# Loading the second half of the weights in 4-KB runs, in tiles of two modes by 256 rows, contracted behind all attention

## Chip, cores, metric

One core of one Trainium2 chip. The metric is the time of one execution in microseconds (us) on the device, median of several runs. The kernel before takes 467.04 us (runs from 466.96 to 467.75).

## The reference, cut to what matters

Attention with a decay for 8 batches and 8 heads (sequence 576, head size 64), then a spectral mix: the first 64 modes of the Fourier transform along the sequence are multiplied by a complex 512 x 512 matrix of their own, and transformed back.

```python
x = attention(q, k, v, f).transpose(0, 2, 1, 3).reshape(8, 576, 512)
X = np.fft.rfft(x, axis=1)[:, :64]
Yr = einsum('bmd,mde->bme', Xr, w_r) - einsum('bmd,mde->bme', Xi, w_i)
Yi = einsum('bmd,mde->bme', Xr, w_i) + einsum('bmd,mde->bme', Xi, w_r)
u = x + np.fft.irfft(Y, n=576, axis=1)
out = u + np.maximum(u @ w_ch, 0)
```

`w_r` and `w_i` are 64 x 512 x 512 floats each, 134 MB in all: each weight is read once and used for 8 batches only. q, k, v are 28 MB, the output 9 MB.

## The kernel before

The 32 steps of attention (4 pairs of heads, called dc, times 8 batches) each load q, k, v on the SyncE queue. The weights come as 64 tiles of 4 modes x 128 rows, real and imaginary part in one transfer each, cast to bf16 on the way, through a ring of 9 buffers, on the queue that POOL (the GpSimd engine) feeds. A row of a weight matrix is 512 floats: one contiguous run of 2 KB per mode and partition.

```python
    MG = 4
    NG = NM // MG
    # ... cut ...
    NRING = 9
    # ... cut ...
    def emit_w_load(n):
        dc, g = tile_of(n)
        wb = wpool.tile([128, 2, MG, D], BF16, tag="wb", name="wb")
        parts = 2 if n == NDC * NG - 1 else 1
        for h in range(parts):
            ms = slice(h * MG // parts, (h + 1) * MG // parts)
            for t, src in enumerate((moe_w_r, moe_w_i)):
                nc.gpsimd.dma_start(
                    wb[:, t, ms, :],
                    src[g * MG : (g + 1) * MG, dc * 128 : (dc + 1) * 128, :][
                        ms
                    ].rearrange("m p e -> p m e"),
                )
        wtiles[n] = wb
    # ... cut ...
    def emit_modes(n):
        dc, g = tile_of(n)
        wb = wtiles.pop(n)
        XT3 = XT3s[dc]
    # ... cut ...
        for mi in range(MG):
            m = g * MG + mi
            for eb in range(NDC):
                for t, c0 in ((0, B), (1, 0)):
                    nc.tensor.matmul(
                        A[:, eb, mi, :],
                        lhsT=wb[:, t, mi, eb * 128 : (eb + 1) * 128],
                        rhs=XT3[:, m, c0 : c0 + 2 * B],
                        start=(t == 0),
                        stop=(t == 1),
                    )
        ysl = Yacc[:, :, g * MG : (g + 1) * MG, :]
        if dc == 0:
            nc.vector.tensor_copy(ysl, A[:, :, :, :])
        elif dc < NDC - 1:
            nc.vector.tensor_tensor(ysl, A[:, :, :, :], ysl, ALU.add)
```

The last of the four dc passes adds into `YT` (or `YTl` for the 16 modes that come last), the finished spectrum as the next step reads it, instead of `Yacc`. In the loop over attention steps, two tiles are contracted per step from the ninth step on; `emit_dft` makes the Fourier coefficients of one 128-row block of d:

```python
        for s in range(NS + 1):
            if s + STG - 1 < NS:
                emit_loads(s + STG - 1)
    # ... cut ...
            if s >= 1:
                emit_dft(s - 1)
                vaugs.pop(s - 1)
            if s > B:
                for j in range(2):
                    emit_modes(2 * (s - B - 1) + j)
                    next_w()
        nmode = 2 * (NS - B)
```

The last 16 tiles follow behind attention, beside the blocks `emit_xw` (x times w_ch) and, once `YT` is complete, the eight blocks `emit_y`. After the very last tile comes the output phase ("tail": `emit_late`, `emit_x`, `emit_out`).

```python
            nx = ny = 0
            last = NDC * NG
            while nmode < last - 1:
                emit_modes(nmode)
                nmode += 1
                if nmode <= last - GL:
                    if nx < B:
                        emit_xw(nx)
                        nx += 1
                    next_w()
                if nmode > last - GL:
                    for _ in range((3, 3, 1)[nmode - (last - GL) - 1]):
                        emit_y(ny)
                        ny += 1
            emit_y(ny)
```

The softmax here doesn't subtract the row's maximum and nothing guards it: scores larger than these inputs give would overflow.

## Time and profile before

| | before |
|---|---|
| median time | 467.04 us |
| span in the profile | 466.2 us |
| last weight transfer landed | 422.0 us |
| from there to the end ("tail") | 44.2 us |
| last write of x_all (end of attention) | 331.6 us |
| weights where they are alone, bf16 written | 207 GB/s (414 GB/s read) |

The rows below the first come from one profiled execution. It took 468.06 us, 0.3 us more than the slowest timed run.

The first fence is from the page of the kernel before: rows over the span (the granted TensorE clock in tenths, the busy tenths of the 16 DMA engines, GB/s in 40 slices of 11.7 us), the packets, and the shares of the chain that ended last.

```profile
PEclk9988999997577667776757766669559999889998
DMA  8999999999999999999999999999999999992667
GB/s 187 268 268 268 268 268 268 267 267 253 233 236 236 235 234 231 229 235 230 232 236 237 235 226 206 207 206 206 207 207 206 207 207 206 207 177 79 229 245 270
DMA packets 93235, 106.27 MB, mean 228 GB/s; under 512 B 4032, under 2 KB 88512, under 8 KB 93184
...
DMA 89%; PE 5%; ACT 2%; issue 1%; DVE 1%; POOL 1%; DVEq 0%; ACTq 0%; POOLq 0%
```

The DMA row is at 9 up to 420 us (8 in the first slice): the transfers are never idle. The GB/s row tells who uses them: 268 with q, k, v and weights together, 207 from 280 us on with weights alone. The chain of waits is 89% DMA.

The chain in order of time shows the pace of the transfers: start, duration, what. Each hop spans eight weight transfers (POOL issues one when the one eight earlier has landed), then 0.28 us until the next.

```profile
324.54 20.06 DMA wb<-in_moe_w_i_dram
344.60 0.28 issue
...
406.94 15.01 DMA wb<-in_moe_w_i_dram
422.00 0.55 PE A L111 x15
...
423.24 0.40 PE pl L645 x4
423.69 0.82 PE pl L649 x3
```

So eight transfers of 1 MB read take 20.06 + 0.28 = 20.34 us, 2.54 us each. The last landing releases PE at 422.00; what follows is the tail.

The windows view gives busy time of PE (TensorE, matmuls), weight loads, DVE (VectorE), ACT (ScalarE) and POOL, then the granted clock, DMA share and GB/s of a stretch:

```profile
core 0: us, PE busy (x) PEld busy (x) DVE busy (x) ACT busy (x) POOL busy (x), PEclk, DMA share, GB/s
60.00:100.00 40.00, 33.71 (x669) 27.14 (x671) 36.22 (x99) 39.47 (x62) 6.37 (x9) 1.00 1.16 268
100.00:140.00 40.00, 26.46 (x499) 22.58 (x500) 21.83 (x61) 22.03 (x34) 7.63 (x11) 0.72 1.19 244
404.00:411.00 7.00, 4.26 (x43) 2.48 (x45) 1.03 (x2) 0.59 (x1) 1.40 (x2) 0.51 1.24 206
411.00:422.00 11.00, 10.13 (x138) 6.42 (x138) 4.20 (x9) 4.09 (x7) 0.00 (x0) 1.00 0.84 140
```

(The DMA share can exceed 1 because the records of packets overlap in time.) Up to 100 us ACT is full; after it attention waits for weights (ACT 22 of 40 us). And the y blocks, which run from 407.9 to 420.0 us, keep PE busy 10.1 of 11 us before the last landing: the tail starts at full clock.

### The profile page before, as it was taken

The numbers are of one execution on the slowest core, as the hardware profiler recorded it, in microseconds if no ns is written. First come the engines' busy times: TensorE is split into PE (matmuls) and PEld (weight loads), VectorE is DVE, ScalarE is ACT, GpSimd is POOL, SyncE is SP. The second block draws the span as 40 slices with busy tenths as digits, with TensorE's granted clock in tenths as the row PEclk, the third lists the DMA queues.
The fourth block names the chain that finished last, engine by engine and source line by source line (L and its number), as shares of the span: only waits on it lengthen the run. The fifth ranks groups of instructions, "written<-read, shape, count | busy, mean of one in ns | idle before, by whom it ended". The sixth has DMA issues, their size and how long they took to land.

```text
span 466.2 us, 11413 instructions
## 1 busy us (share of the span) xinstructions
PE 321.9 (69%) x4800; PEld 236.0 (51%) x4845; DVE 250.9 (54%) x625; ACT 250.7 (54%) x376; POOL 123.4 (26%) x154
## 2 busy tenths in 40 slices
PE   1667777996655655565565566776369999597993
PEld 1445556775544544454555455665346555453441
DVE  7767898995444445553544445655223233235774
ACT  4778999995444445554444445654004444134763
POOL 6111100311212222122222222322233222300884
PEclk9988999997577667776757766669559999889998
DMA  8999999999999999999999999999999999992667
GB/s 187 268 268 268 268 268 268 267 267 253 233 236 236 235 234 231 229 235 230 232 236 237 235 226 206 207 206 206 207 207 206 207 207 206 207 177 79 229 245 270
DMA packets 93235, 106.27 MB, mean 228 GB/s; under 512 B 4032, under 2 KB 88512, under 8 KB 93184
## 3 DMA queue, kind: packets, MB, share of 16 engines
q0 software_dynamic: 68144, 67.64, 87.0%
q1 hardware_dynamic: 24960, 37.77, 25.4%
q8 instruction: 38, 0.62, 0.5%
q10 hardware_dynamic: 80, 0.13, 0.2%
q14 instruction: 13, 0.11, 0.1%
HBM read 163.73 MB, written 9.44 MB: 371 GB/s over the span
## 4 chain that ended last, share of the span: by engine, by line
DMA 89%; PE 5%; ACT 2%; issue 1%; DVE 1%; POOL 1%; DVEq 0%; ACTq 0%; POOLq 0%
DMA wb<-in_moe_w_i_dram 69%; DMA wb<-in_moe_w_r_dram 12%; DMA wch<-in_moe_w_ch_dram 8%; PE pz L674 2%; PE pu L686 1%; PE pz L686 1%; ACT uo L702 1%; ACT uo L699 0%; PE pu L669 0%; PE pl L649 0%; POOL wb L86 0%; DVE uo L703 0%; DVE uo L696 0%; DVEq L755 0%; PE pl L645 0%
## 5 line engine op out<-in xcount | busy, mean ns | idle before, releaser
L111 PEld LDWEIGHTS <-wb 128*128 128x128 bf16 x2048 | 67.2, 100 | 109.3 <-DMA wb<-in_moe_w_i_dram 88.0
L86 POOL DMA_DIRECT2D wb<-in_moe_w_r_dram x65 | 48.3, 743 | 188.3 <-DMA wb<-in_moe_w_r_dram 103.6
L86 POOL DMA_DIRECT2D wb<-in_moe_w_i_dram x65 | 48.3, 742 | 116.4 <-DMA wb<-in_moe_w_i_dram 112.4
L437 ACT ACTIVATE E_129<-ps 128x1024 bf16<-128x1024 f32 x64 | 54.3, 875 | 12.0 <-PE ps L430 10.6
L437 ACT ACTIVATE E_128<-ps 128x1024 bf16<-128x1024 f32 x64 | 53.9, 867 | 7.8 <-PE ps L430 7.6
L111 PE MATMUL A<-XT_1367,wb 128*128 128x16 bf16 x512 | 21.1, 174 | 40.6 <-DMA wb<-in_moe_w_i_dram 33.9
L122 DVE TENSOR_TENSOR Yacc<-A,Yacc 128x256 f32<-128x256 f32 x32 | 14.1, 441 | 64.1 <-PE A L111 63.4
L591 ACT CAST XW<-pxw 128x512 bf16<-128x512 f32 x40 | 22.7, 586 | 39.2 <-PE pxw L584 39.2
L111 PE MATMUL A<-XT_2872,wb 128*128 128x16 bf16 x512 | 20.4, 174 | 28.6 <-DMA wb<-in_moe_w_i_dram 26.0
L584 PE MATMUL pxw<-wch,yy 128*128 128x512 bf16 x152 | 36.7, 391 | 1.9 <-DVE yy L580 1.6
L384 ACT COPY KTz_0_126<-tp 64x576 bf16<-64x576 bf16 x16 | 10.9, 680 | 43.9 <-PE tp L375 43.9
L700 POOL TENSOR_TENSOR uo<-uo 64x512 f32<-64x512 f32 (+1 forms) x14 | 25.2, 1808 | 27.5 <-DVE uo L696 24.7
L384 ACT COPY KTz_0_124<-tp 64x576 bf16<-64x576 bf16 x16 | 10.3, 644 | 40.7 <-PE tp L375 40.6
L473 DVE TENSOR_TENSOR x_all<-pav,rcp 128x384 bf16<-128x384 f32 x64 | 31.1, 486 | 0.4
L464 PE MATMUL pav<-va,E_128 128*128 128x65 bf16 x480 | 26.3, 215 | 6.6 <-PE px L488 1.8
L126 DVE TENSOR_TENSOR YT<-A,Yacc 128x256 bf16<-128x256 f32 x12 | 7.3, 611 | 42.1 <-PE A L111 42.1
L111 PE MATMUL A<-XT_454,wb 128*128 128x16 bf16 x512 | 18.1, 171 | 16.9 <-DMA wb<-in_moe_w_i_dram 13.1
L464 PE MATMUL pav<-va,E_129 128*128 128x65 bf16 x480 | 27.3, 216 | 3.6 <-PE px L488 2.0
L430 PE MATMUL ps<-QTs,KTz_0_124 128*128 128x512 bf16 (+2 forms) x96 | 27.6, 341 | 2.9 <-ACT E_129 L437 1.8
L430 PE MATMUL ps<-QTs,KTz_0_126 128*128 128x512 bf16 (+2 forms) x96 | 26.6, 333 | 2.5 <-ACT E_128 L437 2.1
L464 PEld LDWEIGHTS <-E_128 128*128 128x128 bf16 x480 | 23.7, 113 | 8.8 <-issue 2.8
L464 PEld LDWEIGHTS <-E_129 128*128 128x128 bf16 x480 | 24.4, 114 | 5.0 <-issue 3.0
(138 smaller groups left out, 740.2 us busy)
## 6 DMA issues: line engine op xcount, KB each, us to landing
wb<-in_moe_w_r_dram POOLq DMA_DIRECT2D x63, 512.0 KB, 24.8
wb<-in_moe_w_i_dram POOLq DMA_DIRECT2D x63, 512.0 KB, 25.1
out_dram<-uo SPq DMA_DIRECT2D x16, 512.0 KB, 3.0
stq_113<-in_q_dram SPq DMA_DIRECT2D x11, 288.0 KB, 8.4
stk_114<-in_k_dram SPq DMA_DIRECT2D x11, 288.0 KB, 8.2
stv_115<-in_v_dram SPq DMA_DIRECT2D x11, 288.0 KB, 8.7
stq_116<-in_q_dram SPq DMA_DIRECT2D x11, 288.0 KB, 9.6
stk_117<-in_k_dram SPq DMA_DIRECT2D x11, 288.0 KB, 9.6
```

Source lines behind the costliest of these rows:

```text
L86: nc.gpsimd.dma_start(wb[:, t, ms, :], src[g * MG : (g + 1) * MG, dc * 128 : (dc + 1) * 128, :][ms].rearrange("m p e -> p m e"),)
L111: nc.tensor.matmul(A[:, eb, mi, :], lhsT=wb[:, t, mi, eb * 128 : (eb + 1) * 128], rhs=XT3[:, m, c0 : c0 + 2 * B], start=(t == 0), stop=(t ...
L122: nc.vector.tensor_tensor(ysl, A[:, :, :, :], ysl, ALU.add)
L384: nc.scalar.copy(KTz[s % NK][h][hs, 0:S].rearrange("c (p r) -> c p r", r=NR), tv[hs, :, :],)
L430: nc.tensor.matmul(ps[:, h, o : o + n], lhsT=KTz[s % NK][h][:, jb * 128 : (jb + 1) * 128], rhs=QT[s][:, jb * 128 + c0 : jb * 128 + c0 + n] ...
L437: nc.scalar.activation(E[:, :, piece * 512 : piece * 512 + w], ps[:, :, 0:w], ACT.Exp, scale=scale,)
L464: nc.tensor.matmul(pav[:, i, h, :], lhsT=E[:, h, c : c + 128], rhs=va[:, jb, h, :], start=(jb == 0), stop=(jb == sb),)
L473: nc.vector.tensor_tensor(x_all[:, b, sbs[0] : sbs[0] + n, dc * 128 : (dc + 1) * 128].rearrange("p c (h d) -> p c h d", h=2), pav[:, 0:n, ...
L584: nc.tensor.matmul(pxw[:, :], lhsT=xT[:, eb, sb * 128 : (sb + 1) * 128], rhs=wch[:, eb, :], start=(eb == 0), stop=(eb == NDC - 1),)
L591: nc.scalar.copy(XW[:, b, sb, :], pxw[:, :])
L674: nc.tensor.matmul(pz[:, i, :], lhsT=ident_bf[:, :], rhs=XW[:, b, sb0 + i, :], start=True, stop=False,)
L700: nc.gpsimd.tensor_tensor(o_sb, o_sb, u_sb, ALU.add)
```

## The change

Intent: fewer, longer runs. Two neighbouring rows of a weight matrix are 4 KB in a piece. If partition p holds rows 2p and 2p+1 of the second half of d (256 rows), the runs double. That needs the coefficients of even and odd rows (a DFT with a stride of 2 in d) and contracts both dc passes in one, which is possible only when attention is done for all heads. So the first 32 tiles stay as they were, now spread over the 24 steps (4/3 per step in place of 2), and 32 new tiles of 2 modes x 256 rows come behind attention.

```diff
-    xtpool = ctx.enter_context(tc.tile_pool(name="xtpool", bufs=2))
+    xtpool = ctx.enter_context(tc.tile_pool(name="xtpool", bufs=3))
+    NT = NDC * NG
+    NTH = NT // 2
+    M2 = MG // 2
+    GL = 8
     # emit_w_load, second half:
+            wb = wpool.tile([128, 2, M2, 2 * D], BF16, tag="wb", name="wb")
+                    nc.gpsimd.dma_start(
+                        wb[:, t, ms, :],
+                        src[g * M2 : (g + 1) * M2, D // 2 : D, :][ms].rearrange(
+                            "m (p r) e -> p m (r e)", r=2
+                        ),
+                    )
     # emit_modes, second half:
+            terms = [
+                (XT3s[2 + r], r, t, c0) for t, c0 in ((0, B), (1, 0)) for r in (0, 1)
+            ]
     # emit_dft: nothing at dc == 2; at dc == 3 two blocks of stride 2
+            for c, d0, st in [(dc, dc * 128, 1)] if dc < 2 else [(2, 256, 2), (3, 257, 2)]:
     # the attention loop
-                for j in range(2):
-                    emit_modes(2 * (s - B - 1) + j)
+                while nmode < (s - B) * NTH // (NS - B):
+                    emit_modes(nmode)
     # behind attention
-                if nmode > last - GL:
-                    for _ in range((3, 3, 1)[nmode - (last - GL) - 1]):
+                if nmode % 4 and nx < B:
+                    emit_xw(nx)
+                if nmode > last - 6 and ny < B - 1:
+                    for _ in range(2 if ny < 4 else 1):
                         emit_y(ny)
```

(To make room, ident_f and ones_row move into Yacc's space, trimask and wdec into the attention's pool, and vb has one buffer.)

More of the change, by code (lines that the diff above doesn't have):

```diff
@@ L63 @@
     ident_bf = const.tile([128, 128], BF16, name="ident_bf")
-    ident_f = const.tile([128, 128], F32, name="ident_f")
-    trimask = const.tile([128, 128], BF16, name="trimask")
     wch = const.tile([128, NDC, D], BF16, name="wch")
@@ L68 @@
     BI = const.tile([128, SP], BF16, name="BI")
-    wdec = const.tile([128, NSB, BH], BF16, name="wdec")
-    wdec6 = const.tile([RP, NR, BH], BF16, name="wdec6")
     wtiles = {}
-    GL = 4
+    NT = NDC * NG
+    NTH = NT // 2
+    M2 = MG // 2
+    GL = 8
     def tile_of(n):
-        dc, g = divmod(n, NG)
-        return dc, (g + GL) % NG if dc == NDC - 1 else g
+        if n < NTH:
+            return divmod(n, NG)
+        return 2, (n - NTH + GL) % NTH
     def emit_w_load(n):
         dc, g = tile_of(n)
-        wb = wpool.tile([128, 2, MG, D], BF16, tag="wb", name="wb")
-        parts = 2 if n == NDC * NG - 1 else 1
-        for h in range(parts):
-            ms = slice(h * MG // parts, (h + 1) * MG // parts)
+        if n < NTH:
+            wb = wpool.tile([128, 2, MG, D], BF16, tag="wb", name="wb")
             for t, src in enumerate((moe_w_r, moe_w_i)):
                 nc.gpsimd.dma_start(
-                    wb[:, t, ms, :],
-                    src[g * MG : (g + 1) * MG, dc * 128 : (dc + 1) * 128, :][
-                        ms
+                    wb[:, t, :, :],
+                    src[
+                        g * MG : (g + 1) * MG, dc * 128 : (dc + 1) * 128, :
                     ].rearrange("m p e -> p m e"),
                 )
+        else:
+            wb = wpool.tile([128, 2, M2, 2 * D], BF16, tag="wb", name="wb")
+            parts = 2 if n == NT - 1 else 1
+            for h in range(parts):
+                ms = slice(h * M2 // parts, (h + 1) * M2 // parts)
+                for t, src in enumerate((moe_w_r, moe_w_i)):
+                    nc.gpsimd.dma_start(
[4 more added lines that the diff above has]
+                    )
         wtiles[n] = wb
@@ L98, in emit_modes @@
         wb = wtiles.pop(n)
-        XT3 = XT3s[dc]
+        nm = MG if n < NTH else M2
         if late["psM"] is None:
             z = late["psZ"].tile([128, 2, D], F32, tag="z", name="A")
-            A = z[:, 0, 0 : NDC * MG * 2 * B].rearrange(
-                "p (e m c) -> p e m c", e=NDC, m=MG
-            )
-        else:
-            A = late["psM"].tile([128, NDC, MG, 2 * B], F32, tag="A", name="A")
-        for mi in range(MG):
-            m = g * MG + mi
+            A = z[:, 0, 0 : NDC * nm * 2 * B].rearrange(
+                "p (e m c) -> p e m c", e=NDC, m=nm
+            )
+        else:
+            A = late["psM"].tile([128, NDC, nm, 2 * B], F32, tag="A", name="A")
+        if n < NTH:
+            terms = [(XT3s[dc], 0, t, c0) for t, c0 in ((0, B), (1, 0))]
+        else:
+            terms = [
+                (XT3s[2 + r], r, t, c0) for t, c0 in ((0, B), (1, 0)) for r in (0, 1)
+            ]
+        for mi in range(nm):
+            m = g * nm + mi
             for eb in range(NDC):
-                for t, c0 in ((0, B), (1, 0)):
+                for i, (XT3, r, t, c0) in enumerate(terms):
                     nc.tensor.matmul(
                         A[:, eb, mi, :],
-                        lhsT=wb[:, t, mi, eb * 128 : (eb + 1) * 128],
+                        lhsT=wb[:, t, mi, r * D + eb * 128 : r * D + (eb + 1) * 128],
                         rhs=XT3[:, m, c0 : c0 + 2 * B],
-                        start=(t == 0),
-                        stop=(t == 1),
-                    )
-        ysl = Yacc[:, :, g * MG : (g + 1) * MG, :]
-        if dc == 0:
+                        start=(i == 0),
+                        stop=(i == len(terms) - 1),
+                    )
+        ysl = Yacc[:, :, g * nm : (g + 1) * nm, :]
+        if n < NG:
             nc.vector.tensor_copy(ysl, A[:, :, :, :])
-        elif dc < NDC - 1:
+        elif n < NTH:
             nc.vector.tensor_tensor(ysl, A[:, :, :, :], ysl, ALU.add)
         else:
-            n8 = MG * 2
+            n8 = nm * 2
             yt, w = (late["YTl"], GL * n8) if g < GL else (late["YT"], 2 * NM)
@@ L129, in emit_modes @@
                 ),
-                _strided(A[:, 0, 0, 0:1], [[MG * 2 * B, NDC], [1, B], [B, n8]]),
+                _strided(A[:, 0, 0, 0:1], [[nm * 2 * B, NDC], [1, B], [B, n8]]),
                 _strided(
-                    Yacc[:, 0, g * MG, 0:1], [[NM * 2 * B, NDC], [1, B], [B, n8]]
+                    Yacc[:, 0, g * nm, 0:1], [[NM * 2 * B, NDC], [1, B], [B, n8]]
                 ),
@@ L157 @@
         )
+        trimask = ssb.tile([128, 128], BF16, name="trimask")
+        wdec = ssb.tile([128, NSB, BH], BF16, name="wdec")
+        wdec6 = ssb.tile([RP, NR, BH], BF16, name="wdec6")
         NK, NE = 2, 2
@@ L197, in scratch @@
             )
+        ident_f = scratch(128, 128)
         ftf = scratch(128, S)
@@ L265 @@
         nc.vector.tensor_copy(cumT[:64, 4, :], cum_ps[:64, 4, :])
-        ones_row = const.tile([1, 128], F32, name="ones_row")
+        ones_row = scratch(1, 128)
         nc.vector.memset(ones_row[:], 1.0)
@@ L364, in emit_transposes @@
             )
-            vb = qkb.tile([RP, NR, 2, Dh], BF16, tag="vb", name="vb")
+            vb = qkb.tile([RP, NR, 2, Dh], BF16, tag="vb", name="vb", bufs=1)
             nc.vector.tensor_tensor(
@@ L483, in emit_dft @@
             dc, b = steps[s]
-            if b == 0:
-                XT3s[dc] = xtpool.tile([128, NM, 3 * B], BF16, tag="XT3", name="XT3")
-            px = psT.tile([128, NM, 2], F32, tag="tr", name="px")
-            for sb in range(NSB):
-                nc.tensor.matmul(
+            if dc == 2:
+                return
+            for c, d0, st in [(dc, dc * 128, 1)] if dc < 2 else [(2, 256, 2), (3, 257, 2)]:
+                if b == 0:
+                    XT3s[c] = xtpool.tile(
+                        [128, NM, 3 * B], BF16, tag="XT3", name=f"XT{c}"
+                    )
+                px = psT.tile([128, NM, 2], F32, tag="tr", name="px")
+                for sb in range(NSB):
+                    nc.tensor.matmul(
+                        px[:, :, :],
+                        lhsT=_strided(x_all[:, b, sb, d0 : d0 + 1], [[st, 128]]),
+                        rhs=bas[:, sb, :, :],
+                        start=(sb == 0),
+                        stop=(sb == NSB - 1),
+                    )
+                XT3 = XT3s[c]
+                nc.vector.tensor_copy(
+                    _strided(XT3[:, 0, B + b : B + b + 1], [[3 * B, NM], [B, 2]]),
                     px[:, :, :],
-                    lhsT=x_all[:, b, sb, dc * 128 : (dc + 1) * 128],
-                    rhs=bas[:, sb, :, :],
-                    start=(sb == 0),
-                    stop=(sb == NSB - 1),
-                )
-            XT3 = XT3s[dc]
-            nc.vector.tensor_copy(
-                _strided(XT3[:, 0, B + b : B + b + 1], [[3 * B, NM], [B, 2]]), px[:, :, :]
-            )
-            nc.scalar.mul(XT3[:, :, b : b + 1], px[:, :, 1:2], -1.0)
+                )
+                nc.scalar.mul(XT3[:, :, b : b + 1], px[:, :, 1:2], -1.0)
         NS = len(steps)
         nload = NRING
+        nmode = 0
         def next_w():
@@ L533 @@
             if s > B:
-                for j in range(2):
-                    emit_modes(2 * (s - B - 1) + j)
+                while nmode < (s - B) * NTH // (NS - B):
+                    emit_modes(nmode)
+                    nmode += 1
                     next_w()
-        nmode = 2 * (NS - B)
     with ExitStack() as bctx:
@@ L542 @@
         raw = xtpool.tile([128, NM, 3 * B], BF16, tag="XT3", name="YTl")
-        nl = 2 * GL * MG
+        nl = 2 * GL * M2
         YTl = (
@@ L551 @@
         yy = bsb.tile([128, B, 2, D], BF16, name="yy")
-        nc.vector.memset(YT[:, :, :, 0 : 2 * GL * MG], 0.0)
+        nc.vector.memset(YT[:, :, :, 0 : 2 * GL * M2], 0.0)
         yflat = yy[:, :, :, :].rearrange("p b t e -> p (b t e)")
@@ L611 @@
             nx = ny = 0
-            last = NDC * NG
+            last = NT
             while nmode < last - 1:
@@ L615 @@
                 nmode += 1
-                if nmode <= last - GL:
-                    if nx < B:
-                        emit_xw(nx)
-                        nx += 1
-                    next_w()
-                if nmode > last - GL:
-                    for _ in range((3, 3, 1)[nmode - (last - GL) - 1]):
+                next_w()
+                if nmode % 4 and nx < B:
+                    emit_xw(nx)
+                    nx += 1
+                if nmode > last - 6 and ny < B - 1:
+                    for _ in range(2 if ny < 4 else 1):
                         emit_y(ny)
```

## The prediction

> **What bounds the kernel now.** Transfers. The chain of waits is 89% DMA, hops ending on weight transfers from 3.5 to 422.0 us; then a tail of 44 us (PE, ACT, DVE, stores) that no load hides. The slice rows show DMA at 9 tenths nearly throughout. Weights, written as bf16, move at 207 GB/s where they are alone (280 to 400 us): 414 GB/s read. In the windows view PE and ACT are busy about 60% and 50% from 100 to 280 us: attention waits for weights. Only before 100 us is ACT full (39.5 of 40 us), and there DMA is full too (268 GB/s with q, k, v).
>
> **What the change does.**
> - Bytes, matmuls and weight loads stay. The second half of the weights (67 MB read) comes in 4-KB runs in place of 2-KB, with half the descriptors.
> - Attention consumes 32 tiles in place of 48, so it ends near 250 us in place of 335; the other 32 are contracted behind it. The DMA sum is the same: this alone saves nothing.
> - Ring: at 6.1 us a step (as at 60 to 100 us) a step uses 1.33 tiles and DMA brings about 0.65 beside q, k, v. The ring of 9 drains before attention ends, so DMA never lacks a free buffer. Behind attention, 8 XW blocks with 11 tiles cost PE about 60 us, in which DMA brings 12 tiles; the ring takes that.
> - One vb buffer, strided DFT loads, smaller evacuations: off the critical path.
>
> **Cost.** In the chain 8 weight transfers take 20.05 + 0.28 us: 2.54 us per 1 MB read, 32 runs on each of 16 engines, 79 ns per 2-KB run. The Trainium skill, "DMA: Bandwidth & Descriptors" (section Bandwidth), gives 32-byte beats at 850 MHz and about 3 cycles fixed per packet: (64+3)/0.85 = 78.8 ns, which this trace agrees with. A 4-KB run is then (128+3)/0.85 = 154 ns, an estimate from that page: 2.2 to 2.6% less. 64 transfers x 0.06 us = 3.7 to 4.2 us saved on the critical path.
>
> Against it: the eight y blocks run now between 406 and 420 us and warm PE's clock (granted 0.51 at 404 to 411, 1.00 at 411 to 422). The instruction order hoists them three or four tiles earlier; after them PE does 1 us of modes per 5 us, so the tail probably starts cold. "TensorE: Matmul & The Clock Gate" (Part 1) gives a window of about 3.4 us before the clock doubles; 3 us of matmuls at half rate cost an estimated 1 to 2 us. The last evacuation is half the size: -0.2 us.
>
> Sum: 467.0 - 4.0 + 1.3 - 0.2 = **464.1 us**, range 460.5 to 467.0. Faster by over 2%: 0.05; within 2%: 0.92; slower: 0.03.
>
> **What the profile would show.**
> - Software queue about 16,000 packets fewer; weights alone at 211 to 213 GB/s from about 255 us on.
> - Last x_all write near 250 us, q, k, v ended before; DMA at 9 until the last weight lands near 418 us.
> - Tail 45 to 46 us, granted clock near 0.5 in its first 3 us.
>
> **What would make it wrong.**
> - 4-KB runs get split, or another limit sets the rate: 467 to 468.
> - Fewer descriptors also relieve slow DMA engines (the weight rate fades from 414 to 421 us, engines finishing unevenly): 2 to 3 us more.
> - Attention over 9 us a step by itself, or PE behind after it: full ring, idle DMA, slower.
> - PE stays warm: 1.3 us faster.

## The result

| | before | changed |
|---|---|---|
| median time | 467.04 us | 464.98 us (464.76 to 465.33) |
| span in the profile | 466.2 us | 463.0 us |
| last weight transfer landed | 422.0 us | 417.4 us |
| tail | 44.2 us | 45.6 us |
| last write of x_all | 331.6 us | 253.6 us |
| weights alone, written | 207 GB/s | 211 GB/s |

The ratio is 0.9953 (95% interval 0.9936 to 0.9970). It is the mean time of one kernel's fast runs over that of the other's of the same rounds, so not quite the ratio of the medians. A later repeat, beside the experiments, gave 0.9954 (465.53 us against 467.27). The gain is half a percent: by the bound of 2% "the same", but clear of noise.

The page of the changed kernel, same lines:

```profile
PEclk9979999999987887579899599998555558657998
DMA  8999999999999999999999999999999999982667
GB/s 205 268 268 268 268 268 268 267 267 267 268 266 228 232 258 240 246 217 264 208 206 208 211 212 211 211 211 211 211 211 211 211 211 211 211 161 83 225 245 267
DMA packets 76852, 106.28 MB, mean 230 GB/s; under 512 B 4032, under 2 KB 55744, under 8 KB 76800
...
DMA 88%; PE 6%; ACT 1%; issue 1%; DVE 1%; POOL 1%; DVEq 0%; ACTq 0%; POOLq 0%
```

There are 16,383 packets fewer, at the same MB, and 211 GB/s in place of 207 from the slice at 280 us on. The DMA row is as full as before: neither the earlier end of attention nor the ring let the transfers idle. The granted clock, however, sits at 5 in the slices from 320 us on, but for a short rise.

The chain of the changed kernel:

```profile
302.35 19.60 DMA wb<-in_moe_w_i_dram
...
402.75 14.67 DMA wb<-in_moe_w_i_dram
...
417.46 0.55 PE A L130 x14
...
418.46 0.61 PE pl L674 x4
419.07 1.71 PE pl L678 x4
```

A hop of eight takes 19.60 + 0.28 = 19.88 us: 2.485 us per transfer in place of 2.54, so 56 to 57 ns less, and about 3.6 us over the 64 transfers of the second half. The last two lines are the price: the first transposes of the tail take 0.61 us (before 0.40) and the matmuls after them 1.71 us for four (before 0.82 us for three).

```profile
core 0: us, PE busy (x) PEld busy (x) DVE busy (x) ACT busy (x) POOL busy (x), PEclk, DMA share, GB/s
100.00:140.00 40.00, 32.42 (x669) 26.30 (x668) 33.24 (x92) 35.60 (x54) 6.08 (x8) 0.96 1.16 266
391.30:394.70 3.40, 2.39 (x42) 1.32 (x39) 1.22 (x3) 1.14 (x2) 0.71 (x1) 1.00 1.12 213
394.70:398.10 3.40, 1.70 (x33) 1.18 (x34) 0.42 (x1) 0.59 (x1) 0.91 (x2) 1.00 1.11 209
411.00:417.00 6.00, 3.47 (x52) 2.10 (x52) 0.36 (x1) 0.00 (x0) 0.00 (x0) 0.50 0.57 106
417.00:422.00 5.00, 4.08 (x26) 2.07 (x27) 0.85 (x3) 0.57 (x1) 0.00 (x0) 0.50 0.01 3
```

In the stretch from 100 to 140 us attention now runs on (ACT 35.6 of 40 us, before 22.0), because it needs fewer weights per step. At the end of the loads PE idles, and the clock is at 0.50 where it was 1.00. The y blocks ran from 379.0 to 396.1 us, 21 us ahead of the last landing.

### The profile page after: what moved, and what is told of

The parts are those of the page before. It is cut to its first block, busy times and chain, and to the rows that moved or that the text cites. A ratio compares the mean times of both kernels' runs of the same rounds, so it can differ in the third digit from the quotient of the medians.

```text
span 463.0 us, 11454 instructions
## 1 busy us (share of the span) xinstructions
PE 315.8 (68%) x4845; PEld 224.3 (48%) x4845; DVE 245.0 (53%) x625; ACT 248.0 (54%) x376; POOL 120.9 (26%) x154
## 4 chain that ended last, share of the span: by engine, by line
DMA 88%; PE 6%; ACT 1%; issue 1%; DVE 1%; POOL 1%; DVEq 0%; ACTq 0%; POOLq 0%
DMA wb<-in_moe_w_i_dram 69%; DMA wb<-in_moe_w_r_dram 12%; DMA wch<-in_moe_w_ch_dram 8%; PE pz L703 2%; PE pu L715 1%; PE pz L715 1%; ACT uo L731 1%; PE pu L698 1%; PE pl L678 1%; ACT uo L728 0%; POOL wb L87 0%; DVE uo L732 0%; DVE uo L725 0%; DVEq L784 0%; PE pl L674 0%
## 5 line engine op out<-in xcount | busy, mean ns | idle before, releaser
L130 PE MATMUL A<-XT,wb 128*128 128x16 bf16 x2048 | 77.1, 172 | 101.8 <-DMA wb<-in_moe_w_i_dram 74.2
L460 ACT ACTIVATE E<-ps 128x1024 bf16<-128x1024 f32 (+1 forms) x128 | 105.6, 855 | 19.1 <-PE ps L453 17.6
L453 PE MATMUL ps<-QTs,KTz 128*128 128x64 bf16 (+4 forms) x384 | 73.1, 303 | 8.7 <-ACT E L460 7.6
L145 DVE TENSOR_TENSOR YT<-A,Yacc 128x128 bf16<-128x128 f32 x24 | 8.8, 368 | 97.1 <-PE A L130 97.1
L487 PE MATMUL pav<-va,E 128*128 128x65 bf16 x960 | 48.1, 202 | 2.8 <-DVE x_all L496 2.0
L407 ACT COPY KTz<-tp 64x576 bf16<-64x576 bf16 x64 | 42.9, 671 | 7.5 <-PE tp L398 6.6
L475 DVE TENSOR_TENSOR E<-E,trimask 128x256 bf16<-128x256 bf16 (+2 forms) x128 | 38.6, 307 | 11.5 <-ACT E L460 10.6
L487 PEld LDWEIGHTS <-E 128*128 128x128 bf16 x960 | 41.0, 104 | 5.5 <-DVE x_all L496 2.5
L453 PEld LDWEIGHTS <-KTz 128*128 128x128 bf16 x384 | 32.3, 104 | 21.3 <-issue 14.6
L389 DVE TENSOR_TENSOR vb<-stv,wdec 96x768 bf16<-96x768 f32 x32 | 30.4, 950 | 3.4 <-PE tp L398 3.4
L413 DVE COPY QTs<-tp 128x576 bf16<-128x576 bf16 x32 | 24.1, 752 | 5.3 <-PE tp L398 4.1
```

Of the source, the lines that this page charges most:

```text
L130: nc.tensor.matmul(A[:, eb, mi, :], lhsT=wb[:, t, mi, r * D + eb * 128 : r * D + (eb + 1) * 128], rhs=XT3[:, m, c0 : c0 + 2 * B], start=(i ...
L389: nc.vector.tensor_tensor(vb[:, :, :, :], stv_[:, :, :, :].rearrange("p h r d -> p r h d"), _strided(wdec6[:, 0, c0 : c0 + 1], [[BH, NR], ...
L407: nc.scalar.copy(KTz[s % NK][h][hs, 0:S].rearrange("c (p r) -> c p r", r=NR), tv[hs, :, :],)
L453: nc.tensor.matmul(ps[:, h, o : o + n], lhsT=KTz[s % NK][h][:, jb * 128 : (jb + 1) * 128], rhs=QT[s][:, jb * 128 + c0 : jb * 128 + c0 + n] ...
L460: nc.scalar.activation(E[:, :, piece * 512 : piece * 512 + w], ps[:, :, 0:w], ACT.Exp, scale=scale,)
L475: nc.vector.tensor_tensor(dg, dg, tr, ALU.mult)
```

## Experiments

The theory had two terms: a fixed cost per run of the transfers (gain), and a cold TensorE clock (granted 0.50 in place of 1.00) at the start of the tail (loss). Rivals: order, one pass or placement in memory make the gain; other things about the late tiles lengthen the tail. Times below are medians, with the ratio to the kernel before of the same rounds.

### e1a and e1b: run length alone

These two kernels differ in the run length, and with it in which rows a partition holds. Both use one transfer per mode: twice as many, of half the size.

```diff
 # e1a
-                        src[g * M2 : (g + 1) * M2, D // 2 : D, :][ms].rearrange(
-                            "m (p r) e -> p m (r e)", r=2
+                    rows = src[g * M2 + mi, D // 2 : D, :]
+                        rows.rearrange("(p r) e -> p (r e)", r=2),
 # e1b: partition p takes rows p and p + 128; DFT blocks contiguous again
+                        rows.rearrange("(r p) e -> p r e", r=2),
+            ... else [(2, 256, 1), (3, 384, 1)]:
```

> The changed kernel, but each second-half load split in two, one mode each (twice the transfers, half the size, runs still 4 KB). It is the control for e1b. Run-length theory: only one more completion descriptor per engine and transfer, so at most +0.5 us: 465.0 to 465.5 us, last weight landing 417.5 to 418. Rival (the size or number of transfers sets the rate): landing later by 2 us or more, 467 us or more.

> As e1a (order, one pass, number of transfers), but partition p takes rows p and p+128, so runs are 2 KB again. Run-length theory: 3.6 to 4.2 us slower than e1a, about 469 us, landing near 421.7, weights alone back at 207 GB/s. Rival (order, one pass, smaller evacuations, or the start of the run gave the gain): within 0.7 us of e1a.

Measured: e1a 468.33 us (ratio 1.0018), e1b 470.36 us (1.0058). The chains, e1a first:

```profile
359.10 9.74 DMA wb<-in_moe_w_i_dram
...
419.10 0.56 PE A L127 x14
```

```profile
391.85 9.96 DMA wb<-in_moe_w_i_dram
...
422.38 0.56 PE A L127 x14
```

With the 0.28 us after each hop, eight of these half transfers take 10.02 us in 4-KB runs and 10.24 us in 2-KB runs, and the last landing moves from 419.1 to 422.3 us: 3.3 us for the run length alone (3.5 us by the pace: 0.22 us times 16 hops), a little below the 3.6 to 4.2 expected. The rival (order, one pass) would have shown nothing. The difference of the totals is only 2.0 us, because e1a's program closes late: it ends 2.6 us after its last store has landed, where e1b and the changed kernel take 0.9 us. That was seen in its one profiled run, which is also its median run. What it waits for there I did not find; the landing is free of it.

e1a missed its own expectation (465.0 to 465.5), half of it by the late close. The other half: twice the number of transfers moved the landing by 1.6 us (417.4 to 419.1). Over 62 additional transfers that is 26 ns each; against the second look at the changed kernel (landing 417.9, see e6) it is 18, and by the pace 20 (two of e1a's transfers take 2.505 us, one of the changed kernel's 2.485). The +0.5 us that I had allowed for is 8. Each transfer ends with one packet of 4 bytes per DMA engine; the trace of the changed kernel has 2,096 of them in the software queue, of 19 ns on average.

### e2: runs of 8 KB (wrong result on purpose)

```diff
-                        src[g * M2 : (g + 1) * M2, D // 2 : D, :][ms].rearrange(
-                            "m (p r) e -> p m (r e)", r=2
+                    rows = src[g, :, :].rearrange("(p r) e -> p r e", r=4)
```

> Wrong result on purpose: each second-half tile reads all 512 rows of one mode, four rows per partition, so runs are 8 KB at the same bytes, transfers and matmuls. From 2.54 us (2 KB) and 2.485 us (4 KB) per transfer, the fixed cost of a run is about 3.5 ns. Theory of a fixed cost per run: 28 ns less per transfer, 64 of them, -1.8 us: 463.2 us, landing 415.7. Rivals (runs are cut at 4 KB, or the bytes themselves are the limit at 4 KB): unchanged, 465.0 us.

Measured: 463.68 us (0.9912), result wrong as intended, landing 415.8 us.

```profile
301.76 19.38 DMA wb<-in_moe_w_i_dram
...
415.83 0.56 PE A L131 x14
```

19.36 to 19.38 + 0.28 us per eight: 2.458 us per transfer. The landing is within 0.1 us of the one expected. The runs are not cut at 4 KB: the trace has 7,936 packets of 4,096 bytes written (8 KB read).

All five kernels can be put into one sum. The Trainium skill's page "DMA: Bandwidth & Descriptors", section Bandwidth, gives beats of 32 bytes, a fabric of 850 MHz and a fixed overhead of about 3 cycles per packet. Put together, which is an estimate from that page, a run of n beats takes (n + 3)/0.85 ns. To this come 20 ns more per transfer, which are fitted:

| kernel | runs per engine | measured per transfer | sum |
|---|---|---|---|
| before | 32 of 2 KB | 20.34/8 = 2.542 us | 32 x 78.8 + 20 = 2.542 |
| changed | 16 of 4 KB | 19.88/8 = 2.485 us | 16 x 154.1 + 20 = 2.486 |
| e2 | 8 of 8 KB | 19.66/8 = 2.458 us | 8 x 304.7 + 20 = 2.458 |
| e1a | 8 of 4 KB | 10.02/8 = 1.253 us | 8 x 154.1 + 20 = 1.253 |
| e1b | 16 of 2 KB | 10.24/8 = 1.280 us | 16 x 78.8 + 20 = 1.281 |

With this one fitted term, the estimate from the page's figures agrees to about a nanosecond per transfer. The doubled transfers of e1a and e1b show the 20 ns (two of them take 20 and 18 ns more than one whole transfer of the same runs). That the closing packet is what takes them is the likely reading, not a shown one: the records of data packets, too, are each some 19 ns longer than the sum's figure for their run (98, 173 and 324 ns between 300 and 400 us), so packets overlap on record, and the 19 ns of a closing packet need not be 19 ns of pace.

### e3 and e8: y blocks late

```diff
+        n = {55: 60, 60: 55}.get(n, n)      # tile_of, second half
         return 2, (n - NTH + GL) % NTH
-                if nmode > last - 6 and ny < B - 1:
-                    for _ in range(2 if ny < 4 else 1):
+                if nmode > last - 4:
+                    for _ in range((3, 3, 1)[nmode - (last - 4) - 1]):
```

The y blocks need tile 55, so exchanging it with tile 60 pins them beside the last three tiles.

> The changed kernel with tiles 55 and 60 exchanged, so that the eight y blocks can only run beside the last three tiles, as before the change. Clock theory: granted clock 1.00 before the last weight lands, tail 44.2 us in place of 45.6, time 463.5 us, landing unchanged at 417.5. Rival (the longer tail has another cause, such as the smaller late tiles): tail stays 45.6, 465 us, or y blocks now hold up the last tiles: slower.

Measured: 464.06 us (0.9915). The same kernel again as e8, beside the changed kernel on one chip:

> The kernel of e3 again, beside the changed kernel on one chip. Clock theory: 0.8 us faster than it (tail 1.5 us shorter, last tile's matmuls 0.7 us later), 464.1 us. Rival: equal.

> The changed kernel again, for a comparison on one chip with e7 and e8: 465.0 us, landing 417.5, tail 45.6 with the clock at 0.5 for some 4 us after the landing.

Measured: e8 463.90 us (0.9920), the changed kernel 465.53 us (0.9954): 1.6 us faster, twice what was expected. From the end of the last matmuls on weights to the end of the program e8 takes 43.6 us and the changed kernel beside it 45.3: the clock's 1.5 us and a little more. But those matmuls end only 0.1 us later in e8, not 0.7, since the changed kernel's last weights landed 0.4 us after e8's (417.9 against 417.5). That 0.4 us is spread of the landing and not the clock. The windows view of e3, columns as above:

```profile
411.00:418.00 7.00, 6.93 (x84) 4.22 (x84) 2.50 (x7) 2.93 (x5) 0.00 (x0) 1.00 0.50 93
```

The clock is at 1.00 before the landing, and from the end of the last matmuls on weights it takes 43.65 us to the end of the program (before 43.62, changed 45.05). In e3 those matmuls end at 418.7 us rather than 418.0: the last weights landed 0.3 us later (417.7), and some 0.4 us go to the y blocks, which are in their way. So e3's time from the landing to the end is 44.6 us, where 44.2 was expected.

### e4: busy work in place of moved work

The order of the y blocks stays early (all are emitted before), and after tiles 60, 61 and 62 ten matmuls run whose result nobody reads.

```diff
+                if nmode > last - 4:
+                    for _ in range(10):
+                        pd = psBig.tile([128, D], F32, tag="big", name="pd")
+                        nc.tensor.matmul(
+                            pd[:, :], lhsT=wd[:, 0, 0, 0:128], rhs=wd[:, 0, 0, 0:D],
+                            start=True, stop=True,
+                        )
```

> The changed kernel; its y blocks stay early, but ten matmuls of 512 columns, whose result nobody reads, are added after each of the tiles 60, 61 and 62, to keep PE busy up to the last landing. Clock theory of the longer tail: granted clock 1.00 at the landing (417.5), first transposes and matmuls of the late rows back at 0.40 and 0.82 us in place of 0.61 and 1.71, tail 44.2 us, 463.5 us in all. Rival (the order of the y blocks itself or the smaller late tiles lengthen the tail): tail 45.6 or longer, 465 us or more.

Measured: 464.78 us (0.9939, interval 0.9926 to 0.9952), runs from 463.40 to 465.32. In the profiled run, the fastest of the six, the mechanism is as expected: PE's timeline (start, busy us, operation, count) shows the late rows' transposes back at 0.40 us, and 43.56 us from the end of the weights' matmuls to the end of the program.

```profile
418.58 0.40 PE L684 MATMUL pl<-ident_bf,YTl 128*128 128x128 bf16 x4 [0.46 <-DVE YTl L145]
418.82 1.03 PE L688 MATMUL pl<-wch,YTl 128*128 128x512 bf16 x4
```

So in this run the clock explains all of the longer tail, not the order of the blocks or the size of the late tiles: here both are as in the changed kernel. As a way to gain time it is poor. The median missed by 1.3 us, and why the other runs are slower than the profiled one was not settled.

### e5: one tile earlier

As e3 with tiles 55 and 59 exchanged, and `(2, 2, 2, 1)` blocks after the last tiles.

> The changed kernel with tiles 55 and 59 exchanged and two y blocks after each of the last tiles from 59 on: warm as in e3, but with one more tile of time, because in e3 the y blocks held up the last tile's matmuls by 0.7 us. Expected: granted clock 1.00 at the landing, last matmuls on the weights done at 418.0 in place of 418.5, 463.4 us, 0.7 us under e3. Rival (clock falls again before the end, or the blocks still hold up the last tile): 464.1 or more.

Measured: 464.29 us (0.9929). The rival held and the expectation fell. The instruction order put the first matmuls of the next tile ahead of y blocks, so PE waited for that tile with y blocks behind it, and the clock fell at 414.4 us (the windows view, columns as above):

```profile
411.00:414.40 3.40, 1.75 (x39) 1.30 (x39) 0.47 (x3) 0.27 (x2) 0.00 (x0) 1.00 0.73 137
414.40:418.00 3.60, 3.60 (x21) 1.64 (x20) 0.81 (x2) 0.91 (x2) 0.00 (x0) 0.53 0.35 64
```

PE was busy 1.75 of 3.4 us in the window before the fall.

### e6 and a second look at the kernel before: the start

The profile of before reached the landing of w_ch (the tenth load) at 97.5 us, the changed kernel at 96.0. That could be the moved constants.

> The kernel before, with only the change's moves in memory (ident_f and ones_row into Yacc's space, trimask and wdec into the attention's pool, one vb buffer, a third XT buffer). In the changed kernel and all its variants wch landed at about 96.1 us, before at 97.5. If the placement does that, 465.6 us and wch at 96.1. If it is chance or comes from elsewhere, 467.0 us.

> The kernel before, unchanged, for a second profile of its start. If the late start is its own: wch lands at 97.5 again and the first weight transfer at about 11.9 us. If it was chance: about 96.1 and 9.4.

Measured: e6 468.27 us (1.0014): the moves in memory give nothing (wch at 97.1). The second look at the kernel before (467.3 us, a single run) has wch at 97.2 and its last weight landing at 421.1 us, 0.8 us before that of the first profile. The second look at the changed kernel (465.46 us in the profiled run) has wch at 97.1, as late as the kernel before, and lands its last weight at 417.9. The hops that end the loads of these two, the kernel before first:

```profile
406.04 15.10 DMA wb<-in_moe_w_i_dram
```

```profile
403.25 14.67 DMA wb<-in_moe_w_i_dram
```

So the earlier w_ch is no fixed property of the changed kernel, whose two looks differ by 1.0 us there. Its variants, from e1a to e8, lie between 95.8 and 96.8, so a tendency remains; a cause was not found, and the sum below needs none. The landings spread by 0.8 us in the kernel before and 0.5 us in the changed one, and the gain between them is 3.2 to 4.5 us, depending on which two profiles are compared. The pace of the hops, which does not depend on this spread, is the better measure.

### e7: both findings in one correct kernel

Modes 0 to 31 come behind attention as tiles of one mode by all 512 rows (four rows per partition, 8-KB runs); modes 32 to 63 in 2-KB runs in four passes, three of them during attention; y blocks as in e3. Its core:

```diff
+            dc, g = divmod(n, GH)                   # first half: modes 32 to 63
+            return dc, NH + g * MG
+        n = {47: 60, 60: 47}.get(n, n)              # second half: one mode each
+        return 0, (n - NTH + GL) % NH
+                        src[m0, :, :].rearrange("(p r) e -> p r e", r=4)[:, :, es],
+            if dc == NDC - 1:                       # emit_dft: four blocks of stride 4
+                todo += [(4 + r, r, 4, 0) for r in range(4)]
```

> A correct kernel built on what e2 and e3 showed: modes 0 to 31 come behind attention as tiles of one mode by 512 rows (four rows per partition, 8-KB runs), modes 32 to 63 in 2-KB runs as before, three quarters of them during attention; y blocks late as in e3. Run-length theory: landing at about 415.9, 1.6 us before that of the changed kernel (512 runs per engine saved, 3.2 ns each), clock 1.00 at the landing; the last matmuls end about 0.7 us after it more than in the changed kernel: 462.3 us. Rival (24 in place of 32 tiles used in attention fill the ring, or five DFT blocks a step hold attention up): DMA idle, 464 us or more.

Measured: 462.21 us (0.9888, interval 0.9872 to 0.9903), correct: 3.3 us under the changed kernel of the same rounds and 5.1 us under the kernel before. The total is as expected, but not by the parts expected. The profiled run is the slowest of the four, 462.98 us, 0.8 us over the median, so some of what follows may be that run's own. The landing is at 417.0, not 415.9; the last matmuls end at 417.8, only 0.8 us after it; the clock is warm and 43.5 us follow. The last tile is cut into 1-KB runs (to let its first half start early), which by the sum above costs about 0.3 us of the 1.1; the rest is open. DMA was not idle.

## Why the prediction was right, point by point

The prediction (464.1 us, range 460.5 to 467.0) holds the measured 464.98 us, and both of its mechanisms were shown. The range is wide: its upper end is the time of the kernel before. What bears the prediction out is the parts.

- **Runs.** Predicted 3.7 to 4.2 us on the critical path. Measured 3.6 us by the pace of the chain, 3.3 us by e1a against e1b, 3.2 to 4.5 us by the landings. The middle of the forecast was too large by some 0.4 us: the step "2.54 us per 1 MB read, 32 runs on each of 16 engines, 79 ns per 2-KB run" charged everything to the runs, but some 20 ns of a transfer come once per transfer, and the change does not save them. That the page's 78.8 ns fitted the 79 ns so well hid it; e1a's doubled transfers uncovered it.
- **Cold tail.** Predicted +1 to 2 us, less 0.2. Measured 45.6 - 44.2 = +1.4 us net (+1.6 in the second look); e3, and e4 in its profiled run, take it away by warming the clock. The y blocks were in fact hoisted further than I read from the order: the last ended 21 us ahead of the landing. With the smaller evacuation (0.37 us in place of 0.62) included, the gross cost is about 1.7 us.
- **Moving half of the weights behind attention saves nothing by itself.** Shown: attention ended 78 us earlier (253.6 us; forecast 250) and the DMA row stayed full. e1b has all of the move and none of the runs, and its last landing is at 422.3 us; less the 1.6 us of its doubled transfers that is 420.7, 0.4 us from the second look at the kernel before (421.1) and 1.3 us from the first (422.0, the slower run). An effect of the move under about a microsecond is not excluded.
- **The ring.** It never filled for long enough to let the transfers idle (up to 79.5 us POOL waited 20.7 us for a buffer to come free, but the DMA row was at 9 meanwhile); XW behind attention was taken up, as forecast.
- **Slow DMA engines.** The possible extra of 2 to 3 us did not come: the rate still fades over the last 6 us (106 GB/s between 411 and 417 us).

Sum: -3.6 + 1.4 = -2.2 us; measured -2.1 us by the medians, -1.7 us in the repeat. The forecast of -2.9 us was off by 0.8 us: 0.4 us too much for the runs, 0.3 us too little for the tail, the remainder rounding.

## What to carry to other kernels

Where transfers are the bound and never idle, only their own time counts: count runs and transfers, take the cost of each from two sizes rather than dividing one duration by one of the counts, and leave the order of the work alone unless it makes a buffer or an engine wait. A gain there may be given back right behind it: look at what the engine that starts the next phase did in the microseconds before, because work moved away from there took its warm clock along. And when a phase starts on the last landing, keep real work for just before it, as the three y-block versions did with more or less success.

## What the Trainium skill lacked or had wrong

- The Trainium skill's page "DMA: Bandwidth & Descriptors", Anatomy of one DMA: it calls the bubble of the semaphore write tiny, about one cycle. Here a transfer costs each engine about 20 ns beyond its runs: by the pace 20 ns (e1a) and 18 ns (e1b) for each additional transfer. Which part of that is the write of the closing packet is not shown.
- The same page, Bandwidth: its fixed overhead of about 3 cycles per packet, for which it gives a packet of 256 bytes as the only example, fits here up to runs of 8 KB: 2.542, 2.485 and 2.458 us per transfer of 1 MB in runs of 2, 4 and 8 KB, so 3.4 to 3.6 ns for each run saved.
- "Perfetto Trace Analysis", DMA Optimizations: it says that batching small transfers into larger ones, with 2 KB to 4 or 8 KB as the example, "can dramatically improve throughput". It gives nothing for runs of these sizes inside a large transfer. Here, in transfers of 1 MB read, going from runs of 2 KB to 4 KB was worth 2.2% of the transfers' pace, 8 KB a further 1.1%, and the change half a percent of the kernel's time.
- "TensorE: Matmul & The Clock Gate", Part 1: it says that the clock falls after an idle window of about 3.4 us; how much work a window may hold and still count as idle it does not say. Here the clock fell at 398.1 us in the changed kernel and at 414.4 us in e5 behind 3.4 us in which PE was busy 1.70 and 1.75 us, with no gap over 1.7 us; behind 2.39 of 3.4 us it stayed. So a window need not be empty. A limit cannot be read from these runs: in the changed kernel the clock also fell at 319.6 us, behind 2.62 of 3.41 us busy, and stayed at 176.2 us, behind 2.07 of 3.41.
